# Another order table for the same 2,900 operations of a two-headed kernel (S4D convolution beside linear attention)

## The chip, the cores and the metric

One core of one Trainium2 chip. The metric is the device time in microseconds of one execution of the whole program. Of several runs the median counts. A profile is of one further execution, recorded instruction by instruction.

## The reference, cut to what matters

Two independent halves are computed from separate inputs and laid side by side in the output (2048 rows of 576 + 576 columns):

```python
# half A: a long convolution, by FFT of length 2*L, L = 2048, D = 576 channels, N = 128 states
dt = exp(log_dt);  A = -exp(log_A_real) + 1j * A_imag;  C = (C_real + 1j * C_imag) * dt
K = 2.0 * einsum("dn,dnl->dl", C, exp((A * dt)[:, :, None] * pos)).real
a = irfft(rfft(u.T, 2 * L) * rfft(K, 2 * L))[:, :L].T + u * D_skip
# half B: linear attention with H = 32 heads of 18
q, k, v = split(x @ wqkv)
phi = lambda y: concat([softmax(y @ w_phi), softmax(-(y @ w_phi))])
kv, z = phi(k).T @ v, phi(k).sum()
b = ((phi(q) @ kv) / (phi(q) @ z + 1e-6)) @ wo
return concat([a, b], -1)
```

## The kernel before, in words

All five engines work from one list of about 2,900 operations. `Plan.op` records each operation with its engine (some may run on either of two, ACT or DVE, DVE or POOL), its tiles and its dependences. Nothing is emitted then. At the end `pl.run(ORDER)` walks a long table of numbers, `ORDER`, and emits operation after operation. A number is an operation; `/7` after it names the buffer slot of a tile that the operation touches first, `*` takes the second engine, `!` sets a small activation first so that ACT's function table is loaded early, `+28` puts 28 warming matmuls in front. Each engine takes its instructions strictly in the order in which they were emitted, and waits at each for the tiles it reads and for the slots it writes. So the table decides four things: each engine's order, the order of the DMAs (all issued by SP), which engine takes an operation that has two, and which slot a tile lives in. The slots are few: 8 of PSUM (tile `ps`), 14 large ones (`zi`, `ac`, `x9`, `e`, `ks`, `E`), 19 of a row's size (`v1`, `o`, `ot`, `yo`, `ub`, `kb`, `us`, `zo`, `ff`, `fT`, `mx`), 7 small, 2 each for `pi`, `mg` and `cs`.

The work of half B:
- `fold` multiplies the key and query weights with `w_phi` (wkT or wqT blocks of 126 or 72 rows against the tile `fT` from wphi) and splits each result into a high part `wh` (ACT, L519) and a remainder `wl` (DVE, L520).
- `key_tile(t)`, t = 0 to 15, loads 128 columns of x (tile `zo`), splits them, makes three gemm outputs of 14 matmuls each, takes the two softmaxes (DVE maxima and minima, ACT exponential L598, POOL half sums L601, DVE L602 and L604, POOL product L467), and adds into the `kv` sums.
- `kv` transposes these sums and lays them out as blocks.
- `query_tile(t)` repeats the gemm and the softmax for the queries, transposes the features on TensorE (L705), multiplies them with the kv blocks, divides, transposes again (L735) and multiplies with wo in two halves.

The work of half A:
- `u_first` (16 blocks) is the first FFT stage of u: eight matmul pairs of a 64-row constant `w1` with the tile `kb`, four evictions to `zi`, two stores.
- `params` (6 blocks of 96 channels) prepares phases and angles in small DVE and ACT operations on tiles like `mx`, `mn`, `ax`, `pi`; `mags` does the magnitudes.
- Per pair of groups of four channels, `phases` sums up integers on POOL (L904, five times L908) into a `cs` slot, `waves` makes sines of them on ACT (L918, L925, L926), and `group` multiplies by magnitudes: three size matmuls (`ps` from `sel` and `mg`), exponentials on ACT (L942, L949), products on DVE and POOL, 64 small matmuls (`ps` from `E` and `cs`, L452), which free the `cs` slot, and sums into `ks` on DVE.
- After nine groups `k_first` does the first FFT stage of the kernel: the skip `dsk` is added to `ks`, and four blocks of matmuls (`ps` from `ks` and `w1`, each into four PSUM slots) are evicted to `zi`.
- `product` (16) is the middle of the FFT, the product of the spectra and the way back; `last` (16) is the last stage and the store.

Line 452 is the helper `mm`, through which nearly all matmuls go; lines 457, 460, 467 and 471 are helpers for copies and for products and sums. A TensorE instruction appears as a weight load (PEld) and a matmul (PE).

Of the kernel before, what the change touches and what calls it, by code (L numbers as in the profile page):

```python
# [285 lines left out]
482 1333 52* 1521 1339/1 1252 271/7 275/0 1475 1290/0/4/2/6/6 1514 43/7 53* 1330/8 1293 1207/6 1522 1291 1476 1294*
389 272/3 1328 44 1334 274 276/9 1523/11 278 1331/10 289*/8 1166 56/2 1292 1335 1477 1525 45 73 55/4 390 1336 1337
1340 61/1 1349/3 391/10 1255/0 62 273/7 277 1197/4 279 1518 63/4 59 212/9 58 60 1478 1524 64*/2 1341 1519/1 1351/7
1527 1354 65* 290 57/2 1533 213/10 1479 214* 1338 1520 1199/11 215* 1198 131/12 1347/13 239/14 381/7 240/7 241* 1526
1200/4/3/0/1/11 288 1237/15 1342 1343 1344 392/2 66 1352 1350 67/4 393/1 378/0 398 242* 280*/3 1203 394* 1239/14 132/0  # L290
1345 342/3 217/6 246/0 1204 133* 281* 450/10 1480 477/7 1528 1346 1390/0 395* 68/3 69/2 74 1432/1 1481 399 1529 1202*
218/1 1433 1389 245/3 158/11 70* 1348 1488/2/8/12 216/1 1434 261/4 1201* 1205 75* 1482 224/3 1484/4 1435 71* 1486/7
1483 270/2 221 220 223 54/3 222/13 225 1436 226/2 251/1 263 1489 76 1503/6/4/3 1491 1492 1437 282 262 283/1 1487 250
244/0 347/13 1530 243/4 235/9 1493 1531 1256 219/1 284/3 285/0 234 227 1485 1532 1534 134* 1698 1535/1 138/2 400 286*
228 1238 1536 229/12 348/5 1490 1494 1495/7/2/7 230/3 287 159/10 153/1 1537 1208/12 1538 1438 1504 349 1499/4 428/16
1699 155 247 248 1500 1507 1539 137/2 1540 135/5 252/8 249 253/2 1501/0 1541 231/4 232 254 429/12 1506 1496 1502
401/17 1497 1295 154 1227/15 350 1296 1505 1508 136/6 236 1498 1542 142/2 255 1509 143 237 256/13 1240/7/1/4/3/6 1439
1244* 140 1543 1544 1696 1440 1510/0 1511* 139 352/3 233 1242* 369/14 1177/18 1241 1206 1445/7/3/4 257/3 1545/1 141/11
1443/6 1441 144 258/4 1442 353/2 1217/2 1219/13 238 430* 291* 431 1547/0 1704 356/1 1512 1697 145*/0 1703 160* 1548
359 1705/9 1243 1446! 1447/4 1448 370 434/1 451 355 1549 1550 357/13 146* 147 1551 1451 161 162/6 1513 358 439/0 354/3  # L300
1450 1444 1453 1317/11 361/2 1552 1209* 435/4 1700 1449 1452 360 371 1245 1218 362 259 1246 1553 452 440 441/0
1210/2/7/6/3/1 1211 1214* 363 1213* 432/7 292 1220/2/4/1/0/9 1212* 1223 1707 1222 148/12 149/3 150/2 364/13 365/1 1221
1454/6 1460/4/3/4 1458/2 1461 1546 1462/1 1463 1459 260 264 1467 1466 151 1554 1224 156 366/5 1465 1555 496/16 152
163/7 1464 1468 367 1455* 1556 265 1706 1715 402/8 433/3 368* 1558/4/6/12 1562/2 1708 351/8 1557 455/6 456/5 185/2
1469/0 1709 1710 403* 436 1391/1 166/1 404 1559 1392 1456 1393 437 104/8 1457 442/2 438 1711 157 443 1563 1226 1470
167 168/11 1225 186/9 164/1 169 170 181 1560/3 1561 444 1257/4 1565 171 1394 1566 1395 408/6 425/17 172/2 1712
1575/2/3/4 1564 1471 405/9 1472 1576 1582 1568 1573/1 1583 406/7 1567 1577/0 1396 1216 1574 410/1 1397 445/1 446/0 173
372 407/4 457* 165/3 1701/0 412 458 174 1215 447/5 1178/6 187* 448* 1578 1398 1399 1713 409 1167/9 1579 449 1581 182
411/10 453 175/1 461/2 1404/1/8/1 413 415/5 1580 1402/3 414 1406/7 188* 416 1403! 320/13 466/1 454 1405 1714 1412
1569/0 1259/2 1584/6 1588/0 1589 1590 1411 1702 1570 1571 467 424 1716 1591 460/4 462/1 189/10 1407 1410 417 1717/10  # L310
176/5 478 1592 1258 1593 468/3 105/4 190/2 1400 1355 1572 177/0 1401 1408 178* 1421/3/6/12 423 106* 1718 107 321/0 464
418/10 463 465 1179 469*/5 479 1719 1417/1 179* 1720 1585 1586 1277/12 192/0 419/1 1587 420/2 109/4 1594 1419/6 183
# [24 lines left out]
629 1138/4 1011/4 1139/0 1907 630 631/8 1300/5/1/6/2/11 1301 1681/0 1304 1677/5 1302 1015 1140 1684 1016 536 1690 1678
1691 632/3 1742/1/3/6 1303 1141 1142 1686 1689 633 1147/7/4 537 1682 1687 1148 1145/6/16 1146 1143/2/8 1275 1688 1144
# [821 lines left out]
```

## Time and profile before

| | |
|---|---|
| median of 3 runs | 514.12 us (512.72 to 518.13) |
| the profiled execution | 511.75 us, its span 510.0 us |
| TensorE busy | 496.6 us, 97% of the span |
| DVE busy | 457.5 us, 90% |
| ACT busy | 396.8 us, 78% |
| POOL busy | 334.2 us, 66% |
| granted TensorE clock | 0.999 of full speed |
| moved by DMA | 115.95 MB, 227 GB/s |

The span runs from the first to the last instruction; the rest of the execution lies around it. Busy time of TensorE counts the union of its matmuls, which overlap. A row of the timeline gives the start, the duration, the engine, the source line, the operation, the tiles written and read, their shapes, how many equal instructions the row merges, and in brackets how long the engine had been idle and what ended that.

### The profile page before, as it was taken

The page shows a single profiled execution, that of the slowest core. Times are in us where ns is not written, and L with a number is a line of the kernel's source. Part 1 is how long each engine was busy: PE and PEld are TensorE (multiplying, and loading weights), DVE is VectorE, ACT ScalarE, POOL GpSimd, SP SyncE. Part 2 cuts the span into 40 slices and gives each one's busy share as a digit, 9 for nine tenths or more (in the row PEclk, how much of TensorE's full clock was granted, in tenths as well). Part 3 has the DMA queues.
Part 4 walks back from the last instruction along what each step waited for, and adds up shares of the span by engine and source line. Part 5 has one row for each costly group of instructions (what it writes and reads, how often), then busy time and mean ns, then how long its engine had stood idle before and what let it go on. Part 6 is the DMA issues. An engine that isn't in the chain of part 4 may idle for free.

```text
span 510.0 us, 20296 instructions
## 1 busy us (share of the span) xinstructions
PE 496.6 (97%) x8436; PEld 412.6 (81%) x8436; DVE 457.5 (90%) x1013; ACT 396.8 (78%) x683; POOL 334.2 (66%) x403
## 2 busy tenths in 40 slices
PE   7999999999999999899999999999999999999996
PEld 7799888999998879697887866776788886667976
DVE  4999999999899999999999999998989879789774
ACT  4699787999879989979989889899896445454331
POOL 1645697788987997995994569796554455634400
PEclk9999999999999999999999999999999999999999
DMA  7985947715137586781687965468986997998797
GB/s 212 333 294 178 330 143 252 235 57 170 59 121 254 149 257 207 212 275 58 211 239 255 286 180 181 147 219 272 293 269 213 347 274 219 321 311 295 260 314 193
DMA packets 80511, 115.95 MB, mean 227 GB/s; under 512 B 12452, under 2 KB 57636, under 8 KB 80420
## 3 DMA queue, kind: packets, MB, share of 16 engines
q1 hardware_dynamic: 80420, 114.67, 71.1%
q8 instruction: 66, 1.08, 0.9%
q14 instruction: 25, 0.20, 0.1%
HBM read 65.63 MB, written 49.01 MB: 225 GB/s over the span
## 4 chain that ended last, share of the span: by engine, by line
PE 80%; DVE 7%; ACT 6%; POOL 2%; DMA 2%; issue 2%; SPq 0%; POOLq 0%; DVEq 0%
PE ps L452 75%; PE ps L705 3%; PE ps L735 2%; POOL cs L908 1%; ACT cs L918 1%; DVE E L471 1%; DMA xd<-x 1%; DMA ub<-dram 1%; ACT e L598 1%; DMA fT<-in_wphi_dram 1%; POOL o L601 1%; DVE wl L520 1%; DVE e L467 0%; DVE zi L457 0%; DVE small L602 0%
## 5 line engine op out<-in xcount | busy, mean ns | idle before, releaser
L452 PE MATMUL ps<-wh,x 128*128 128x288 f32 (+2 forms) x1008 | 240.2, 318 | 1.0 <-ACT wh L519 0.4
L452 PEld LDWEIGHTS ps<-wh,x 128*128 128x128 f32 x1008 | 173.0, 188 | 11.8 <-issue 2.8
L452 PE MATMUL ps<-wl,x 128*128 128x288 f32 (+2 forms) x560 | 175.0, 313 | 0.0
L452 PEld LDWEIGHTS ps<-wl,x 128*128 128x128 f32 x560 | 105.3, 188 | 1.2
L908 POOL TENSOR_TENSOR cs<-cs,pi 128x64 int32<-128x64 int32 (+4 forms) x90 | 91.9, 1022 | 5.5
L601 POOL TENSOR_TENSOR o<-e 128x576 f32<-128x576 f32 x32 | 42.4, 1330 | 28.8 <-ACT e L598 22.3
L467 POOL TENSOR_TENSOR E<-v,cs 128x512 f32<-128x512 f32 x31 | 39.5, 1290 | 15.5 <-ACT v L949 12.6
L471 DVE TENSOR_TENSOR ac<-us,ps 128x576 f32<-128x576 f32 x64 | 44.8, 747 | 3.5 <-PE ps L452 2.5
L953 DVE TENSOR_TENSOR cs<-ps,cs 128x1024 f32<-128x1024 f32 x36 | 43.7, 1214 | 2.8 <-ACT ps L942 2.4
L942 ACT ACTIVATE ps<-ps 128x512 f32<-128x512 f32 x72 | 41.6, 591 | 5.1 <-PE ps L452 4.8
L598 ACT ACTIVATE e<-e 128x1152 f32<-128x1152 f32 x32 | 37.4, 1168 | 7.0 <-POOL e L467 4.8
L452 PEld LDWEIGHTS ps<-E,cs 128*32 128x32 f32 x2304 | 34.3, 110 | 10.5 <-issue 5.7
L467 POOL TENSOR_TENSOR e<-small,e 128x576 f32<-128x576 f32 x27 | 31.7, 1173 | 15.7 <-DVE small L467 10.7
L452 PE MATMUL ps<-sel,mg 128*128 128x512 f32 x108 | 40.4, 439 | 1.4 <-DVE e L471 1.0
L452 PE MATMUL ps<-E,cs 128*32 128x64 f32 x2304 | 40.1, 220 | 1.4 <-issue 0.6
L926 ACT ACTIVATE cs<-cs,hp 128x1024 f32<-128x1024 f32 x36 | 40.4, 1141 | 0.0
L925 ACT ACTIVATE cs<-cs 128x1024 f32<-128x1024 int32 x36 | 37.0, 1054 | 0.3
L918 ACT ACTIVATE cs<-cs 128x2048 f32<-128x2048 int32 x18 | 34.4, 1912 | 2.6 <-POOL cs L908 2.5
L457 ACT ACTIVATE zi<-ps 128x288 f32<-128x288 f32 x79 | 28.1, 414 | 8.4 <-PE ps L452 8.4
L467 POOL TENSOR_TENSOR e<-e,small 128x576 f32<-128x576 f32 x25 | 29.7, 1189 | 7.3 <-DVE small L467 6.6
L890 POOL TENSOR_TENSOR pi<-pi 128x192 int32<-128x192 int32 (+1 forms) x42 | 20.0, 486 | 18.9 <-DVE pi L886 16.8
L467 POOL TENSOR_TENSOR ac<-ac 128x288 f32<-128x288 f32 x24 | 19.2, 825 | 18.8 <-DVE ac L471 8.8
(146 smaller groups left out, 1050.0 us busy)
## 6 DMA issues: line engine op xcount, KB each, us to landing
dram<-zi SPq DMA_DIRECT2D x32, 288.0 KB, 4.8
xd<-x SPq DMA_DIRECT2D x16, 576.0 KB, 4.7
dram<-zi SPq DMA_DIRECT2D x16, 576.0 KB, 5.2
x<-xd SPq DMA_DIRECT2D x16, 576.0 KB, 5.6
kb<-dram SPq DMA_DIRECT2D x32, 288.0 KB, 4.6
ub<-dram SPq DMA_DIRECT2D x32, 288.0 KB, 6.2
dram<-zo SPq DMA_DIRECT2D x32, 288.0 KB, 4.4
zi<-dram SPq DMA_DIRECT2D x16, 576.0 KB, 8.8
```

What stands on the lines that cost most here:

```text
L452: pe.matmul(o, l, r, start=start, stop=stop, skip_group_check=skip)
L457: op(("act", "dve"), (c_act(n), c_dve(n)), lambda e: act.activation(dst(), src(), AF.Copy) if e == "act" else dve.tensor_copy(dst(), src() ...
L467: op(eng, [c_dve(n[0]) if e == "dve" else c_pool(n[1]) for e in eng], lambda e: (dve if e == "dve" else pool).tensor_tensor(dst(), a(), b( ...
L471: op(eng, c_dve(n) if eng == "dve" else c_pool(n), lambda: e.tensor_tensor(dst(), a(), b(), op=alu), r=r, w=w, with_=with_, lock=eng == "p ...
L598: op("act", c_act(1152) + 40, lambda: act.activation(e.t, e.t, AF.Exp), r=[e], w=[e], table="exp")
L601: op("pool", c_pool(517), lambda: pool.tensor_tensor(pair.t, e.t[:, :, :, 0:9], e.t[:, :, :, 9:18], op=ALU.add), r=[e], w=[pair], lock=True)
L908: op("pool", c_add(4 * n * W), lambda n=n, j=j: pool.tensor_tensor(x()[:, :, :, n:2 * n], x()[:, :, :, 0:n], pi.t[:, j:j + 2, gs].bitcast( ...
L918: op(("act", "dve"), (c_act(n) + 45, c_dve(n)), lambda e: act.activation(cs.t[:, 0], x(), AF.Abs) if e == "act" else dve.scalar_tensor_ten ...
L925: op("act", c_act(64 * W) + 150, lambda at=at: act.activation(at(1), at(1).bitcast(I32), AF.Sin, scale=TURN), r=[cs], w=[sine], with_=[cs] ...
L926: op("act", c_act(64 * W) + 225, lambda at=at: act.activation(at(0), at(0), AF.Sin, scale=-TURN, bias=hp.t), r=[cs, hp, sine], w=[both], w ...
L942: op("act", c_act(512) + 12, lambda: act.activation(ps.t, ps.t, AF.Exp), r=[ps], w=[ps], table="exp")
L953: op("dve", c_dve(64 * W), lambda: dve.tensor_tensor(F(), both(M.t), F(), op=ALU.mult), r=[M, ready], w=[long], with_=[cs])
```

## The change

`ORDER` is replaced by another table of the same 2,900 operations; nothing else changes. It came out of a search that set out from the current table, with the longest delays and the largest steps that the search allows. The first lines of both:

```diff
 ORDER = """
-180/0 33 0/0 1 1353 3 1358 2 1360 1362 72/1 1361 1366 396/2 1365 1368 1367/3 1369 1370 1371 1372 4/4 35+28/0 1359 1373
...
+369/0 1361 1360 1365 1366 1368 1367/1 1369 1370 1371 1372 1373 1353 0/0 2 450/2 3 477/3 374/4 375/1 1374 1375 4/5 1359
...
```

Operations move by 20 places on average. 174 of those with two engines take the other one: ACT has 643 operations in place of 636, DVE 1011 in place of 1013, POOL 394 in place of 399. Three places in rows; tiles carry the program's running numbers where the names alone would read alike.

SP's first DMAs, at the program's start. Before (tiles from `in_wkT` are weight blocks of the keys, `zo` from `in_xT` is an x tile, `fT` is wphi, the small ones are parameters of block 0):

```order
L508 DMA kvb_83<-in_wkT_dram 72x640
L843 DMA dt_94<-in_ldt_dram 128x96
L845 DMA cre_98<-in_cre_dram 128x96
L845 DMA cim_103<-in_cim_dram 128x96
L504 DMA fT_119<-in_wphi_dram 128x630
L845 DMA th_153<-in_aim_dram 128x96
L508 DMA e_175<-in_wkT_dram 126x640
L508 DMA ub_180<-in_wkT_dram 126x640
L508 DMA e_183<-in_wkT_dram 126x640
L495 DMA zo_185<-in_xT_dram 128x640
L508 DMA e_188<-in_wkT_dram 126x640
```

and now:

```order
L845 DMA cim_83<-in_cim_dram 128x96
L845 DMA cre_85<-in_cre_dram 128x96
L495 DMA zo_113<-in_xT_dram 128x640
L504 DMA fT_119<-in_wphi_dram 128x630
L845 DMA th_121<-in_aim_dram 128x96
L508 DMA kvb_126<-in_wkT_dram 72x640
L843 DMA dt_130<-in_ldt_dram 128x96
L508 DMA e_172<-in_wkT_dram 126x640
L508 DMA e_180<-in_wkT_dram 126x640
L508 DMA ub_182<-in_wkT_dram 126x640
L508 DMA e_212<-in_wkT_dram 126x640
```

The x tile `zo` goes out third in place of tenth, wphi fourth in place of fifth, the 72-row block `kvb` sixth in place of first.

TensorE from the end of query tile 12's gemm to query tile 15's products with kv (`ps` from `kb` is a block of `u_first`, from `sel` a size matmul, from `E` a group, from `ident` the transposes of query 15's features). Before:

```order
L452 MATMUL ps<-wl,x_3547 128x288
L452 MATMUL ps<-kb,w_246 64x288 x8
L452 MATMUL ps<-sel,mg 128x512
L452 MATMUL ps<-E,cs 32x64 x32
L452 MATMUL ps<-sel,mg 128x512
L705 MATMUL ps<-ident,e 128x128 x9
L452 MATMUL ps<-sel,mg 128x512
L452 MATMUL ps<-kvb,fT 64x76 x4
```

and now:

```order
L452 MATMUL ps<-wl,x_3251 128x288
L452 MATMUL ps<-kb,w_257 64x288 x8
L452 MATMUL ps<-sel,mg 128x512 x2
L452 MATMUL ps<-E,cs 32x64 x32
L452 MATMUL ps<-kb,w_257 64x288 x8
L452 MATMUL ps<-sel,mg 128x512 x2
L705 MATMUL ps<-ident,e 128x128 x9
L452 MATMUL ps<-sel,mg 128x512 x2
L452 MATMUL ps<-kvb,fT 64x76 x4
```

A second block of `u_first` (block 0, which stood before the gemm of query 15's second half) now stands ahead of the transposes. The size matmuls are sorted otherwise: two that stood ahead of the second half of query 12's gemm now follow the first block, and of the next group's one has moved behind the transposes and one from behind them ahead.

DVE around the second run of `k_first`, from the sums into `ks` to the evictions. Before (`zi` 4090 is filled from the first block of matmuls; `ks` 2528 and 2529 are the pair of kernel tiles):

```order
L471 TENSOR_TENSOR ks_2528<-ps_3906,ks_2529 128x32x4
L471 TENSOR_TENSOR ks_2528<-ps_4021,ks_2529 128x32x4
L471 TENSOR_TENSOR ks_2529<-ps_3777,ks_2529 128x32x4
L471 TENSOR_TENSOR ks_2528<-ks_2528,dsk_89 128x36
L471 TENSOR_TENSOR ks_2529<-ps_3906,ks_2529 128x32x4
L871 RECIPROCAL mx_4015<-mx_4015 128x96
L457 COPY ot_4008<-ps_4054 128x288
L590 TENSOR_REDUCE small_4104<-ps_3984 128x16
L471 TENSOR_TENSOR mn_4017<-mn_4017,mx_4015 128x96
L457 COPY zi_4090<-ps_4087 128x8x36
```

and now (`ks` 2529 and 2530; `zi` 4092 is filled from the first block, 4115 from the second):

```order
L471 TENSOR_TENSOR ks_2529<-ks_2529,dsk_100 128x36
L471 TENSOR_TENSOR e_4062<-ps_3998,small_4013 128x16x18
L471 TENSOR_TENSOR ks_2530<-ps_3793,ks_2530 128x32x4
L859 SCALAR_TENSOR_TENSOR mx_4066<-ax_3915,ay_3756 128x96
L471 TENSOR_TENSOR ks_2530<-ps_3917,ks_2530 128x32x4
L471 TENSOR_TENSOR x9_3992<-ps_3978,x9_3992 64x128
L471 TENSOR_TENSOR ay_3756<-ay_3756,ax_3915 128x96
L871 RECIPROCAL mx_4066<-mx_4066 128x96
L457 COPY zi_4092<-ps_4089 128x8x36
L471 TENSOR_TENSOR mn_4051<-mn_4051,mx_4066 128x96
L602 TENSOR_REDUCE small_4125<-o_3953 128x64
L457 COPY zi_4115<-ps_4114 128x8x36
```

The sum with `dsk` now stands ahead of the `mx` and `ay` of parameter block 4, and the first eviction `zi` ahead of the product `mn`.

More of the change, by code (lines that the diff above doesn't have):

```diff
@@ L286 @@
[L286 to L300, printed above, removed]
@@ L426 @@
[L426 to L428 removed]
+369/0 1361 1360 1365 1366 1368 1367/1 1369 1370 1371 1372 1373 1353 0/0 2 450/2 3 477/3 374/4 375/1 1374 1375 4/5 1359
+1 1377 33 376* 377* 1358 1362 1363/0 1364 1376 396/6 35+28/0 1378 12/2 1379/4 1380 1381 1382 38 5/3 19/7 34/1 36 37
@@ new lines @@
+429/0 1440 1240/1/3/7/2/1 1507 233 143 144 270/5 1357 1207/10 1317/7 159/4 257/1 1543 1242 1544 160* 1219/6 1244
+145*/2 430* 1441 1241 1277/14 1510/6 1511 401/15 402/9 1705/1 1443/2/5/8 354/3 431 355/4 237* 1547/0 1442 356 258/0
+1447/1 432/6 1448! 1548 1549 291* 1697 357/13 1550 146* 1450 1696 1551 353/0 358 99/11 1243 1245 359 1545 1512 238
+1445/7 1446 1444 1451 371 360 1452 147 1453 370 1208*/18 1552 1553 1449 1209* 1513 1700 259* 351/7 361*/2 362 434/4
+451* 435/3 452 1210/6/2/0/7/12 292 1707 440/4 423/10 1211 1218 1213* 439 441/2 1214 1212 363 148/9 161* 1454/6
@@ new lines @@
+1689 492 1147/4/10 1148 494 493 495 1145/6/18 1143/0/17 1691 2034 1907 1908 1286 634 635 1742/4 1690 1740/1 1146
+1152/6 1018/3 2042 1687 1144 1149/0 2038 1153/4 535/1 1745 1679 1154/17 1150/0 1680 1151 538/11 2035 1019 536 1741
+1692/2 537 2066/1 539 1747 1952/1 1953 640/6/18 1748 641 1746 636/7/10 540 1954 637 1955 638/0/11 1155/6/5 639
+1757/7/6/0 1156/1 1157 1956 1743 1749 1158 1755/3 1750 2036 1159 645/0 1756 642/1 1758 646/0 1759/6 1760 643/4 1957
+1306 1761 2041 1751/4 647/10 1020 1021/11 644 1763 1161/5 697/10 1910/0 1762 648/1/0 1227/18 1228*/10 1163/17 1765
@@ new lines @@
+1866/6/4/0/7/6 704 2060 2219 1971* 1869* 1867* 2061 1868* 703 1917 1164 1920 1973 1032/2 1870* 1871 1035/0 1970*
+1980/4/10/5 705 1033/3 706/0 1036/4 1188*/12 1034/5 855/6 859/3 1872/1/7/3/5/1 1037 1918 860 1875* 1974/0/4/13 1921
+1189* 707 1873* 861/2 1975* 1976 1919 1981 1876* 1175 1038/3/2 1309* 1039/7 1977 2062 2063 2064 1982/6 1983/5 1986*
+1874 1040 1041 854/1 708 1988 892/3 1877 1042 856 857 1230/7/3/6/0/6 1232 1978/2 1979 1985* 1987 858 1231 1234 1233
+1236 709/10 1043/5 1045/5 1310/6/0/7/1/12 1984 862*/4 2224 1989/2 863 1235 1314 710/2 711 1311 1190/6/1/5/4/1
@@ new lines @@
+870/1/12 2069 2225/17 2497/18 871 873* 2470/3/0/6/2/8/7 728 729 876/5 2471 2474* 2473 1047 2070 2071 730 2001 2227
+877/4 2477/2/4/1/3/9/11 2480 2481 2072 874/6/12 2472 2478 875 2226 2235 2228 2073 731/7 733*/7 878/5 2536/3/6/1/0/3/4
+2539* 2540* 2074 732/2 2538 2479 734* 2076 2425/9 2229 2537 2541/6 2543/4/6/0/1/2/10 2075 2221/1 2077 2544
+2482/5/7/2/3/8/2 2484 2446/14 2545 879/4 2006/6/9/11 2486* 2547 940*/4 2230 2231 2546 2004/7 2005 2485 2008/3 894/1
+2019/2/6/1 880/0 881 657 882/4/0 2009/4 2512/15 2010 893/7 2222 2407/16 2007 941 2013 2014 2020 883/7 2023/6 942
@@ new lines @@
+2238 2239 2099 2114 2115 2240 2241 2117 582/6 581/5 586/0 2085* 2116 2454/7 2100* 587 584 588/12 902 2101*
+2526/3/0/2/1/10/15 2527* 583 2242 2118 2487 2528* 2095/4 2096 585 2530* 589/2 590 2089/6 2090* 2529* 957/0 958/3
+2448/5/3/7/1/17/13 2451 2091 959 2092 2452 2450 2102 2449 2554 2103 2453/8 2243 2244 2455/6/0/2/7/2/10 903 736/0 2456
+2121/3/1/6 2122 2245 2246 2457 2123/5 2124/7 2126* 2459 2127* 2119/4 2128 2129 2120 2164/1/5/8 2491/12 2104/6 2490/2
+2165/17 2498/5 2105 591 592/8 2249/0 904/7 2458 888/0 2489/3 2125 890 960/3/1 961/7 2423/11 2492/2/7/5/0/13/14 962
@@ new lines @@
+2260/5 2332 2156* 2333 2158* 2155* 2263! 594 2504/4/3/0/2/14/17 910* 2265/0 2261 2270 2506 2505* 2266 2279/1/4/11
+2398/5 2507* 2431/18 911/7/3 912* 913/4/12 914* 2334 2269 2335 543/3 2336 2147 548 547 2508 595 2280/6
+2426/7/0/5/1/8/1 2430* 2399/4 2429* 2282* 2337 915/6 2555/9 918/1 2427* 916/3 549 2338 2268* 550/4 2433/7/5/4/2/3/9
+919/5 917/3 2510 2267* 2271/3 596 597/6/13 2428 2436 2435 2339 2437 551 599/4/18 920 2275/5 2340 2434 2276 600 2281
+2277/1 2283* 2278 2284 2285 598 552 553/17 2272 2401/2/0/7/4/8/6 2405* 921/6/5 2403 2404 2509 2273 2159 2402* 922/5
@@ new lines @@
+1076/3 2739/3/1/7/5/4/10 2815 792/4/15 2742 1073 2805 2806 2709 2741 2633/16 2671 2672 2808 2746/0/6/2/7/6/5 2740*
+793* 2641/7 2743 2752 2580/5/1/3/4/9/5 2583 2632/2 794/7/11 2751 2753* 2754 2582 2764/10 984 795 2807 2747 2584 692/2
+694/18 2634/17 2581* 2748 2749* 2587/5/4/0/7/13/2 2588 2640/4 2750 2677/6/1/3/2/0/1 2681 2589 798/5 2762/8 2595 2678
+2680 985* 986 2590 2679 2683 2755/3/4/6/2/9/15 2759 2758* 796/0/14 797 2682 2757 693/1 2596 2591 2597 2763/6 695
+2635/7/4/0/6/5/1 2637 2636 801/1 2756* 2761 799/4 2592 2593* 800/16 2770/17 802/4 803 2639* 2771/11 2638
@@ L429 @@
+852 1121/1 1123 1125
 """.split()
```

242 lines of the change are left out of this document (110 added, 132 removed).

## The prediction

> **What bounds the kernel now.** I read the page first (busy time, granted clock, the chain), then busy time by stage, then the rows of the three places where TensorE waits.
>
> ```profile
> span 510.0 us, 20296 instructions
> PE 496.6 (97%) x8436; PEld 412.6 (81%) x8436; DVE 457.5 (90%) x1013; ACT 396.8 (78%) x683; POOL 334.2 (66%) x403
> PEclk9999999999999999999999999999999999999999
> ...
> 5.76:15.36 9.60, 8.90 (x51) 8.19 (x51) 6.77 (x21) 6.07 (x16) 3.37 (x7) 1.00 1.01 293
> 15.36:66.00 50.64, 49.58 (x484) 45.37 (x484) 49.86 (x102) 42.23 (x66) 30.80 (x43) 1.00 0.84 280
> 66.00:165.00 99.00, 98.79 (x1734) 90.14 (x1735) 95.73 (x208) 88.48 (x137) 82.53 (x101) 1.00 0.49 157
> 165.00:204.00 39.00, 38.89 (x797) 32.76 (x798) 37.72 (x85) 37.00 (x59) 34.60 (x42) 1.00 0.70 205
> 204.00:245.00 41.00, 38.47 (x600) 32.06 (x598) 39.84 (x92) 37.18 (x65) 33.98 (x39) 1.00 0.62 187
> 245.00:310.00 65.00, 64.19 (x1295) 51.09 (x1295) 61.03 (x143) 57.94 (x98) 47.70 (x56) 1.00 0.77 236
> 310.00:371.00 61.00, 60.08 (x1354) 43.27 (x1354) 56.12 (x117) 55.81 (x95) 46.92 (x52) 1.00 0.69 220
> 371.00:505.85 134.85, 134.61 (x2133) 106.83 (x2101) 109.29 (x248) 69.69 (x149) 53.48 (x60) 1.00 0.86 277
> ```
>
> The stage rows give length, then busy time of PE, PEld, DVE, ACT and POOL. TensorE has work in 97% of the span, at full clock. An order can't shorten that work; it can only shorten the time in which TensorE has none. From 5.76 to 505.85 us the stages leave it idle for 0.70 + 1.06 + 0.21 + 0.11 + 2.53 + 0.81 + 0.92 + 0.24 = **6.6 us**. Matmuls overlap, so a wait shorter than one of them (about 0.3 us in the rows below) hardly shows; I take as much again for these, an estimate. So all that an order can win inside is 6.6 us shown and perhaps 13 us in truth. The largest piece stands at 204 to 245 us. From 66 to 204 us there is next to nothing to win (0.32 us), though DVE is busy for 133.5 of 138 us there: an order can lose in that stretch, not gain.
>
> What lies outside is a start and an end:
>
> ```profile
> 505.52 0.29 PE L452 MATMUL ps<-wl,x 128*128 128x288 f32 x1
> 505.85 0.41 ACT L457 ACTIVATE ot<-ps 128x288 f32<-128x288 f32 x1 [1.43 <-PE ps L452]
> ```
>
> After the last matmul come one eviction and the last store, 510.0 - 505.85 = 4.15 us. The change ends with the same two gemm halves and the same eviction: **0**. The profiled execution took 511.75 us (510.0 span and 1.75 around it); the median of the runs is 514.12, 2.37 above. I sum against 511.75 and add the sum to 514.12.
>
> **The head: SP's first issues.** The first real matmul needs wphi (tile fT) and the first block of wkT (kvb).
>
> ```profile
> 0.74 0.44 SPq L508 DMA_DIRECT2D kvb<-in_wkT_dram  x1
> 2.60 0.43 SPq L504 DMA_DIRECT2D fT<-in_wphi_dram  x1
> 4.88 0.38 SPq L495 DMA_DIRECT2D zo<-in_xT_dram  x1
> 5.76 2.38 PE L452 MATMUL ps<-fT,kvb 72*128 72x72 f32 x10 [0.97 <-DMA fT<-in_wphi_dram]
> 12.41 0.68 DVE L520 TENSOR_TENSOR wl<-ps,wh 128x504 fp32r<-128x504 f32 x1 [0.38 <-ACT wh L519]
> 12.68 0.59 ACT L519 ACTIVATE wh<-ps 128x504 fp32r<-128x504 f32 x1 [0.18 <-PE ps L452]
> 13.15 1.84 PE L452 MATMUL ps<-fT,e 126*128 126x126 f32 x12 [0.28 <-DVE wl L520]
> 15.36 0.41 PE L452 MATMUL ps<-wh,x 128*128 128x378 f32 x1 [0.37 <-ACT wh L519]
> ```
>
> SP issues one DMA about every 0.46 us here (2.60 to 4.88 in five steps). wphi moves from fifth to fourth, 0.46 earlier; kvb moves from first to sixth, so it goes out near 0.74 + 5 x 0.46 = 3.0 us, 0.4 later than wphi did, which was the later of the two. The first x tile (zo, 128 x 640 floats, 0.33 MB) now goes out third, ahead of every weight: at the 293 GB/s of this stage it costs the weights behind it 1.1 us. So the first fold comes 0.4 to 1.5 us later. But the last wkT block stands eleventh in both orders, behind the same ten transfers. Its ten folds are the end of the run at 13.15, so it had landed by about 13.6. TensorE spent the time from 5.76 on blocks that landed one by one, and a later start eats that waiting. The first gemm (15.36) needs the remainders wl of the first three wkT blocks of 126 rows. The third now stands tenth, one before the last: I place its landing at 12.4 and its folds at 13.8, a block after it; ACT's 0.59 and DVE's 0.68 make 15.1. I take **0**, with -0.5 and +1.5 as ends.
>
> **Place A, query tile 15 (205 to 214 us).**
>
> ```profile
> 193.67 5.20 POOL L908 TENSOR_TENSOR cs<-cs,pi 128x64 int32<-128x64 int32 x5
> 198.90 1.91 ACT L918 ACTIVATE cs<-cs 128x2048 f32<-128x2048 int32 x1
> 204.96 1.28 ACT L949 ACT_TABLE_LOAD   x1
> 207.51 1.18 ACT L598 ACTIVATE e<-e 128x1152 f32<-128x1152 f32 x1
> 209.08 0.43 ACT L457 ACTIVATE zi<-ps 128x288 f32<-128x288 f32 x1
> 208.83 1.31 POOL L601 TENSOR_TENSOR o<-e 128x576 f32<-128x576 f32 x1 [1.03 <-ACT e L598]
> 212.70 0.32 ACT L457 ACTIVATE ks<-ps 128x128 f32<-128x128 f32 x1
> 212.24 1.17 POOL L467 TENSOR_TENSOR e<-e,small 128x576 f32<-128x576 f32 x1
> 208.56 1.72 PE L452 MATMUL ps<-kb,w 32*64 32x288 f32 x16
> 212.00 0.51 PE L452 MATMUL ps<-sel,mg 128*128 128x512 f32 x1
> 213.47 1.20 PE L705 MATMUL ps<-ident,e 128*128 128x128 f32 x9 [0.96 <-POOL e L467]
> ```
>
> The transposes at 213.47 wait for a chain that began at 193.67: POOL's phases of the next group pair, ACT's sines for them, a table load, only then the softmax exponential at 207.51, and POOL's two passes over it. TensorE's own work in that time is shorter than the chain, so its rows from 208.56 on stand apart. The change keeps the steps of the chain in this order on POOL and ACT; one size exponential takes the place of an eviction ahead of the softmax, 0.3 us. TensorE has the same work ahead of the transposes: one size matmul goes behind them and another comes ahead, one u block moves here from further up, and the two kv transposes move behind the group matmul that frees POOL's buffer. A stall that a chain sets doesn't shrink by sorting what stands under it: **0**. Below it may be -0.5, if the buffer comes free earlier. Above it is +1.0: the u block's four evictions, of which DVE had two, are now all on ACT (0.43 each) behind the softmax, and the size matmuls ahead of the transposes need their slots. Nine ACT instructions stand between the exponential and the first of them; nine took 5.2 us before (207.51 to 212.70), so the first starts near 213.0 and the second ends near 213.6.
>
> **Place B, the second key FFT block (228 to 239 us).**
>
> ```profile
> 230.98 1.25 PE L452 MATMUL ps<-ks,w 32*128 32x288 f32 x16 [0.36 <-DVE ks L471]
> 234.28 1.74 PE L452 MATMUL ps<-ks,w 32*128 32x288 f32 x16
> 229.06 5.18 POOL L908 TENSOR_TENSOR cs<-cs,pi 128x64 int32<-128x64 int32 x5
> 232.38 1.98 DVE L471 TENSOR_TENSOR mn<-mn,mx 128x96 f32<-128x96 f32 x1
> 234.29 0.45 DVE L457 COPY zi<-ps 128x288 f32<-128x288 f32 x1
> ...
> L471 DVE TENSOR_TENSOR mn<-mn,mx x6: 245/251/1982, 6.3 to 279.8; 128x96 f32<-128x96 f32 x6
> ```
>
> The second block (234.28) needs PSUM slots that the first one filled. Their eviction (zi at 234.29) stands on DVE behind mn, which took 1.98 us where its kind takes 0.251, until POOL's run of five ended at 234.24. The second block took 1.74 against 1.25, and the first began 0.36 late. In the change DVE adds dsk to ks before the reciprocal's relatives mx and ay, the eviction stands ahead of mn, and the second block writes slots that older tiles left. I follow it by rows: the ks sums end 0.1 to 0.3 earlier, the first block starts at 230.8, the second at 232.5 when ACT has emptied the last slot, both gemm halves behind it run without a wait, and a size matmul waits 0.45 for the first block's last eviction, still behind mn. The same work ends at 238.4, not 239.0: **-0.6**. Ends: -1.8 (all three waits go) and +0.4 (ACT's sines hold the slot as long as mn did).
>
> The Trainium skill's page "SBUF — State Buffer", section "SBUF: two separate sides", says that a DVE instruction with two SBUF inputs and a GpSimd instruction that reads SBUF exclude each other for a whole instruction. The 1.98 us that end with POOL's run agree. By that rule mn is stretched again in the changed kernel, and the sum is the -0.6 above; if the stretch were chance, mn would take 0.25 and the sum would be -1.0.
>
> **The rest.** ACT gets 7 instructions more, DVE 2 and POOL 5 fewer: 3 us of evictions for ACT, which is idle for 113 us. SP's order changes most among the loads for the products of the first half; the tightest of them, product 0's second ub, still follows the matmuls of product 1 that free its slot. For all other places I take **0**: 6.6 - 0.70 - 2.53 = 3.4 us of shown idling could be won, and as much lost.
>
> Sum: 0 (end) + 0 (head) + 0 (A) - 0.6 (B) + 0 (rest) = **-0.6**: 511.2 for a profiled execution like this one, **513.5** for the median.
>
> **Rivals.**
> - *Most of the waits go.* The stages with waits (15 to 66, 204 to 371 us) give back 1.06 + 2.53 + 0.81 + 0.92 = 5.3, and a fifth of the hidden ones 1.3: -6.6, 507.5. For it: 6.6 us is there, and each is a wait of the kind an order can cure. Against it: the largest, place A, is a chain that the order leaves as it was.
> - *ACT becomes what TensorE waits for.* Place: 165 to 245 and 310 to 371 us, where ACT is busy 37.00 of 39, 37.18 of 41 and 55.81 of 61. Evictions moved to it, as at A, queue behind sines and exponentials. It decides from the point where the second of A's moved evictions ends after the softmax is ready, 213.4 us; then every microsecond counts. Price: all four evictions and the 0.3 late, 4 x 0.43 + 0.3 = 2.0 us a stage, 6 in three: 520.1. For it: my count at A is 213.6. Against it: only there do I see it, for 0.2 us.
> - *Nothing at all.* The moves are small (most operations shift by a few places) and fall where TensorE never waited: 514.1.
>
> **How the numbers follow.** About 1% (5.1 us) is what a measurement of this kernel can tell from no change. My forecast with its own range, 510.5 to 516, has 0.45, nothing at all 0.16 within it or just beside it, the waits going 0.22, ACT 0.17. That gives faster 0.22, same 0.61, slower 0.17. The range reaches into both outer cases, 506 to 519.5.
>
> **What would show it.** Right: TensorE's first row with wh stays within 0.5 us of 15.36; the transposes of query 15 still wait for POOL e, near 213 us; the second ks block starts less than 1.6 us after the first; the idle sum of the stages is 5.5 to 7. Wrong: a DMA release of more than 1 us inside the stages after 245 us, ACT as the releaser of PE's longest waits, or an idle sum under 3 or over 10.

## The result: 518.02 us, 0.85% slower, and the profile after

| | before | after |
|---|---|---|
| median of 20 runs each | 513.89 us (510.12 to 518.13) | 518.02 us (514.89 to 522.53) |
| ratio, 95% interval | | 1.0085, 1.0062 to 1.0107 |
| the profiled execution, its span | 511.75, 510.0 us | 516.81, 515.0 us |

On two other chips the ratio was 1.0059 (1.0031 to 1.0086) and 1.0042 (1.0011 to 1.0074). The change makes the kernel slower by 2 to 4 us; I had forecast 0.6 us less.

The page of after, its summary, and busy time by the stages used ahead of it (length, then PE, PEld, DVE, ACT, POOL; the last stage is longer by what the kernel lost):

```profile
span 515.0 us, 20244 instructions
PE 490.9 (95%) x8436; PEld 410.5 (80%) x8436; DVE 453.4 (88%) x1011; ACT 398.4 (77%) x690; POOL 334.8 (65%) x398
...
5.76:15.36 9.60, 6.29 (x57) 6.39 (x58) 4.32 (x17) 5.79 (x12) 2.62 (x6) 1.00 0.94 251
15.36:66.00 50.64, 50.09 (x412) 47.06 (x415) 48.86 (x106) 41.81 (x69) 30.08 (x39) 1.00 0.83 288
66.00:165.00 99.00, 98.51 (x1745) 90.64 (x1734) 96.04 (x210) 88.64 (x138) 80.72 (x99) 1.00 0.46 145
165.00:204.00 39.00, 36.44 (x876) 30.21 (x862) 35.61 (x78) 35.82 (x60) 32.58 (x35) 1.00 0.65 194
204.00:245.00 41.00, 38.54 (x593) 32.96 (x595) 39.14 (x93) 37.99 (x70) 33.72 (x43) 1.00 0.62 181
245.00:310.00 65.00, 64.76 (x1307) 51.74 (x1301) 61.71 (x141) 59.18 (x99) 50.36 (x56) 1.00 0.79 245
310.00:371.00 61.00, 57.57 (x1310) 41.03 (x1310) 53.91 (x116) 54.39 (x91) 44.85 (x50) 1.00 0.68 213
371.00:511.00 140.00, 138.51 (x2211) 110.52 (x2199) 112.68 (x255) 72.61 (x153) 58.98 (x65) 1.00 0.88 279
```

TensorE now idles for 3.31 + 0.55 + 0.49 + 2.56 + 2.46 + 0.24 + 3.43 + 1.49 = 14.5 us, where it was 6.6. Three stages carry most of the rise: the head, 165 to 204, and 310 to 371 us; the last stage adds 1.25.

Idle time alone misses matmuls that start late but overlap. So I matched TensorE's operations of two traces by their numbers in the program, gave each the time that its kind usually takes, and read at equal sums of that work by how many us a kernel stood behind the first profile of before. The first column says when before got there; the three columns on the right are experiments told below (the other slot, the head of before, both):

```
before at    after  again  third   before  | slot   head   head+slot
   us       (three profiles)       again   | (e3b)  (e5)   (e11)
  22.7       2.90   4.34   2.90    1.90    |  2.36   0.94   0.08
  87.0       0.62   2.07   0.64    1.84    |  0.08  -0.36  -1.13
 175.3       1.56   2.85   1.43    4.64    |  0.87   0.27  -0.51
 202.3       4.08   5.43   4.11    5.47    |  3.91   3.03   2.18
 259.6       2.20   3.89   2.39    4.72    |  2.10   1.50   0.59
 350.8       2.05   3.34   1.91    6.20    |  1.36   1.00   0.41
 357.8       4.49   4.56   3.84    6.28    |  1.55   2.87   0.69
 437.2       3.38   3.56   2.72    5.39    |  0.56   1.80  -0.49
 503.2       5.33   4.85   4.63    7.44    |  1.99   3.05   0.85
```

The three profiles of after agree by place: 3 to 4 us lost in the head, about 2.2 won back until 87 us, 2.5 lost between 175 and 202, 1.5 to 1.9 won between 202 and 260, 1.2 to 2.4 lost within 7 us at 355, about 1 won until 437, and 1.3 to 2 lost after that. The column "before again" is the same kernel as the reference of the table, in another execution: this is how far two executions of one program lie apart, and why medians of many runs, not one profile, carry the verdicts below.

Not every step of the table belongs to the change, since the first profile of before was a quick one. I read other profiles in the same way: before again, and those of the experiments that keep before's order at a place. At 22.7 us nine profiles with before's head stand at -0.5 to 1.9 us, seven with after's head at 2.4 to 4.8. From there to 87 us before's order wins at most 0.1. Between 175 and 202 us it loses -0.2 to 1.4, after's order 2.4 to 3.0; between 202 and 260 us it wins 0 to 0.8, and at 355 us it loses nothing. Behind 358 us, though, before's order does as after's does: 0.9 to 1.2 won until 437, 1.5 to 2.2 lost after that. So the five steps that I named up to 358 us are the change's, at least in part; they add up to 3.5 to 4.3 us in the three profiles. The last two steps are not.

**The head.** TensorE's first row in before:

```profile
1.67 3.12 PE L227 MATMUL ps<-ident,zero 128*128 128x126 bf16 x28 [1.67 <-DVE zero L487]
```

and TensorE's rows of after:

```profile
9.07 3.10 PE L227 MATMUL ps<-ident,zero 128*128 128x126 bf16 x28 [9.07 <-DVE ident L485]
11.97 1.43 PE L452 MATMUL ps<-fT,kvb 72*128 72x72 f32 x10
18.68 0.44 PE L452 MATMUL ps<-wh,x 128*128 128x378 f32 x1 [0.28 <-DVE wl L520]
```

and DVE's of after:

```profile
5.88 0.26 DVE L471 TENSOR_TENSOR mn<-mn,mx 128x96 f32<-128x96 f32 x1
7.83 0.26 DVE L859 SCALAR_TENSOR_TENSOR ax<-ax,ay 128x96 f32<-128x96 f32 x1 [1.69 <-ACT ax L849]
8.06 0.18 DVE L1001 MEMSET dsk<- 128x144 f32 x1
8.21 0.11 DVE L487 MEMSET zero<- 128x64 uint32 x1
8.63 0.26 DVE L859 SCALAR_TENSOR_TENSOR ax<-cre,ax 128x96 f32<-128x96 f32 x1 [0.31 <-ACT ax L849]
8.80 0.22 DVE L485 TENSOR_SCALAR ident<-x 128x128 f32<-128x128 int32 x1
```

The 28 warming matmuls read `ident` and `zero`, and every fold stands behind them in TensorE's order. DVE makes both in 0.3 us, but they now stand behind parameter instructions that wait for ACT, which waits for loads, and `ident`, the tenth on DVE, ends at 9.0 us. In before, the warming ran at 1.67, hidden under the loads. The first gemm moves from 15.36 to 18.68 us.

**The slot at 355 us.** ACT and TensorE in the timeline of after, and below them, from its chain of work, the store that ACT waits for:

```profile
350.45 0.73 ACT L457 ACTIVATE us<-ps 128x288 f32<-128x288 f32 x2
352.43 0.89 ACT L460 ACTIVATE x<-ps 128x512 fp32r<-128x512 f32 x2 [1.25 <-DMA dram<-zi]
...
353.81 0.50 PE L452 MATMUL ps<-sel,mg 128*128 128x512 f32 x1 [0.19 <-DVE x L471]
355.08 0.47 PE L452 MATMUL ps<-sel,mg 128*128 128x512 f32 x1 [0.77 <-ACT zo L457]
...
357.94 0.78 PE L452 MATMUL ps<-kvb,fT 128*64 128x76 f32 x16 [1.32 <-DVE small L724]
```

```profile
344.60 7.75 DMA dram<-zi
```

The tile x of query 9 (a transposed output that ACT fills) sits in large slot 5, whose owner before it was a `zi` of the third `k_first`. That tile's store is issued at 344.60 and lands 7.75 us later. Until then ACT stands still, with the evictions that DVE and TensorE wait for behind it.

**Places A and B.** TensorE in after, at query 15's transposes and at the second `k_first`, and there DVE's `mn` and the last of POOL's phase instructions:

```profile
213.50 1.10 PE L452 MATMUL ps<-E,cs 128*32 128x64 f32 x64 [0.73 <-DVE E L471]
215.83 0.80 PE L452 MATMUL ps<-sel,mg 128*128 128x512 f32 x2 [0.55 <-ACT zi L457]
216.53 1.31 PE L705 MATMUL ps<-ident,e 128*128 128x128 f32 x9
...
234.87 2.33 PE L452 MATMUL ps<-ks,w 32*128 32x288 f32 x32
...
236.58 0.25 DVE L471 TENSOR_TENSOR mn<-mn,mx 128x96 f32<-128x96 f32 x1
...
236.62 2.11 POOL L908 TENSOR_TENSOR cs<-cs,pi 128x1024 int32<-128x1024 int32 x1
```

The transposes wait for nothing now; the two waits ahead of them come to 1.28 us. Both `ks` blocks run in one piece of 2.33 us, and `mn` takes 0.25 us.

### The profile page after: what moved, and what is told of

The parts are those of the page before. It is cut to its first block, busy times and chain, and to the rows that moved or that the text cites. A ratio compares the mean times of both kernels' runs of the same rounds, so it can differ in the third digit from the quotient of the medians.

```text
span 515.0 us, 20244 instructions
## 1 busy us (share of the span) xinstructions
PE 490.9 (95%) x8436; PEld 410.5 (80%) x8436; DVE 453.4 (88%) x1011; ACT 398.4 (77%) x690; POOL 334.8 (65%) x398
## 4 chain that ended last, share of the span: by engine, by line
PE 39%; DVE 5%; DMA 5%; ACT 4%; issue 2%; POOL 2%; SPq 0%; DVEq 0%; ACTq 0%; POOLq 0%
PE ps L452 35%; DMA dram<-zi 2%; PE ps L705 2%; DMA ub<-dram 1%; DMA dram<-zo 1%; PE ps L735 1%; DVE ac L471 1%; ACT zi L457 1%; POOL kb L467 1%; DVE zi L457 0%; POOL pi L890 0%; DVE zo L457 0%; ACT x L460 0%; DVE cs L953 0%; ACT cs L926 0%
## 5 line engine op out<-in xcount | busy, mean ns | idle before, releaser
L908 POOL TENSOR_TENSOR cs<-cs,pi 128x64 int32<-128x64 int32 (+4 forms) x90 | 90.8, 1009 | 5.3
L601 POOL TENSOR_TENSOR o<-e 128x576 f32<-128x576 f32 x32 | 44.2, 1381 | 30.9 <-ACT e L598 24.3
L467 POOL TENSOR_TENSOR E<-v,cs 128x512 f32<-128x512 f32 x34 | 43.3, 1290 | 14.7 <-ACT v L949 14.4
L467 POOL TENSOR_TENSOR e<-small,e 128x576 f32<-128x576 f32 x24 | 28.8, 1200 | 13.3 <-DVE small L467 12.4
L467 POOL TENSOR_TENSOR e<-e,small 128x576 f32<-128x576 f32 x26 | 31.2, 1201 | 8.7 <-DVE small L467 8.1
L457 ACT ACTIVATE zi<-ps 128x288 f32<-128x288 f32 x85 | 29.8, 412 | 8.0 <-PE ps L452 8.0
L467 POOL TENSOR_TENSOR ac<-ac 128x288 f32<-128x288 f32 x27 | 21.6, 828 | 20.9 <-DVE ac L471 18.6
```

The costliest lines, as they stand in the source:

```text
L457: op(("act", "dve"), (c_act(n), c_dve(n)), lambda e: act.activation(dst(), src(), AF.Copy) if e == "act" else dve.tensor_copy(dst(), src() ...
L467: op(eng, [c_dve(n[0]) if e == "dve" else c_pool(n[1]) for e in eng], lambda e: (dve if e == "dve" else pool).tensor_tensor(dst(), a(), b( ...
L601: op("pool", c_pool(517), lambda: pool.tensor_tensor(pair.t, e.t[:, :, :, 0:9], e.t[:, :, :, 9:18], op=ALU.add), r=[e], w=[pair], lock=True)
L908: op("pool", c_add(4 * n * W), lambda n=n, j=j: pool.tensor_tensor(x()[:, :, :, n:2 * n], x()[:, :, :, 0:n], pi.t[:, j:j + 2, gs].bitcast( ...
```

## The experiments

Sixteen runs in four groups; each group ran on one chip of its own, beside before. In the diffs, numbers are operations of the table. An interval is about 0.3% wide to either side.

**Ident first.** In after:

```diff
-369/0 1361 1360 ... 1353 0/0 2 450/2 3 ... 1359 1 1377
+369/0 0/0 2 1 1361 1360 ... 1353 450/2 3 ... 1359 1377
```

> The table of after with three operations moved to the front: POOL's iota, DVE's memset of zero and DVE's ident, which the warming matmuls and so the first fold wait for. In after TensorE's first gemm starts at 18.68 us, in before at 15.36. Both theories: the first fold at 6 us in place of 11.97, the first gemm near 15.5. Theory 'the head stays': DVE is busy for 98% of 16 to 86 us, so what is lost ahead of it is never won back; the 3.2 us come off the whole time, 518.0 to 514.8. Rival 'the head is absorbed': the same share of TensorE's work is done only 0.7 us later in after than in before at 78 us, so the lead fades until then; 518.0 to 517.3, and the rest of the loss lies elsewhere.

517.02 us, ratio 1.002 (0.999 to 1.005). The timeline:

```profile
1.51 3.10 PE L227 MATMUL ps<-ident,zero 128*128 128x126 bf16 x28 [1.51 <-DVE ident L485]
7.68 2.38 PE L452 MATMUL ps<-fT,kvb 72*128 72x72 f32 x10 [3.08 <-DMA kvb<-in_wkT_dram]
10.96 4.63 PE L452 MATMUL ps<-fT,e 126*128 126x126 f32 x20 [0.90 <-DMA e<-in_wkT_dram]
18.30 0.44 PE L452 MATMUL ps<-wh,x 128*128 128x378 f32 x1
```

Both theories missed the head itself: the first gemm is at 18.30, not near 15.5. With `ident` out of the way the next thing is late, the loads: `kvb` and the 126-row blocks stand behind the x tile. The two tables of this group that keep after's head whole (below) start their gemm at 20.34 and later, and this one stays 2.0 us ahead of them up to 169 us. The times don't show that: 517.02 stands beside 517.28 and 516.30 of these two.

**Ident late, in before.**

```diff
-180/0 33 0/0 1 1353 3 1358 2 1360 ... 4/4 35+28/0 1359 1373 ... 1375 1376
+180/0 33 0/0 1353 3 1358 1360 ... 4/4 1359 1373 ... 1375 2 1 35+28/0 1376
```

> The table of before with DVE's memset of zero and ident moved behind its tenth parameter instruction (the ax of L859 that reads cre), as in after, and nothing else. Both theories: the first fold waits until about 12 us, the first gemm starts near 18.5. 'The head stays': before + 3.2, 517.1, ratio 1.006. 'The head is absorbed': before + 0.7 at most, 514.6, ratio 1.001.

522.75 us (6 runs), ratio 1.0136 (1.0095 to 1.0177), more than either theory gave. The gemm starts at 20.04 us, and the lag behind the first profile of before is 5.3 us at 22.7 us and 5.3 at 259.6: in this table a late head stays, and nothing is absorbed. The part above 5.3 came behind 260 us, where before again falls back as well.

**The other slot.** In after, large slots 5 and 6 exchanged from operation 922 on:

```diff
-922/5 ... 658/6
+922/6 ... 658/5
```

> The table of after with large slots 5 and 6 exchanged from the feature tile x of query 9 on; the order is untouched. In after that tile sits in the slot of a k_first tile zi whose store lands only at 352.4 us, so ACT stands still for 1.25 us in front of it, DVE 1.59 behind ACT, and TensorE waits 0.19, 0.77 and 1.32 us from 353.8 to 357.9. Theory 'each wait counts': ACT starts the tile near 351.2, the three waits of TensorE shrink to about half a us, and the whole time falls by 1.3 to 2.4, to about 516. Rival 'given back later': what follows is bound by DMA (share 0.88 after 371 us), so the waits go and the time stays at 518.

516.30 us, ratio 0.9996 (0.9965 to 1.0026), in a group without after itself. So it was run again beside after:

> The kernel of after once more, as the measure for the three beside it on this chip. Both theories: ratio 1.006 to 1.0085.

> The slot exchange alone, again, now with after itself on the same chip. Theory 'each wait counts': 2.0 us (0.4%) faster than after, ratio 1.002 to 1.0045. Rival 'given back later': as after, 1.006 to 1.0085; its first ratio of 0.9996 was then the chip's.

After 517.95 us (1.0042, 1.0011 to 1.0074), the other slot 516.89 us (1.0029, 0.9998 to 1.0061). The timeline of the second run:

```profile
350.56 0.94 ACT L460 ACTIVATE x<-ps 128x512 fp32r<-128x512 f32 x2
352.99 0.74 PE L452 MATMUL ps<-sel,mg 128*128 128x512 f32 x2
355.00 0.79 PE L452 MATMUL ps<-kvb,fT 128*64 128x76 f32 x16 [0.21 <-DVE small L604]
```

ACT no longer waits, TensorE's three waits shrink to 0.21, and the lag grows by 0.2 us across this place in place of 1.9 in after of the same group (1.36 to 1.55, against 1.91 to 3.84). The medians differ by 1.06 us; the intervals overlap, so of the time alone the second group tells the slot only as 0 to 0.3%. Shown is the wait and its cause: in the seven profiles with after's slot at this place the lag grows there by 1.2 to 2.4 us, in the seven with the other slot by 0.1 to 0.6.

**The kv transposes.** Two repairs of the stretch from 175 to 202 us. In the first, ACT's split 533 goes behind the four evictions of folds and the transposes (487, 489 and the copy 490) behind `u` block 1270:

```diff
-533 ... 514 ... 487/4 1661 489/2 490*/1 ... 1270/7/5/0/1/5
+514 533 ... 1661 ... 1270/7/5/0/1/5 487/4 489/2 490*/1
```

> The table of after with ACT's split of the first wo piece (L535, which waits 1.59 us for its load at 190.8 us) moved behind the four evictions of folds that stand behind it, and with the two kv transposes moved behind the next u block on TensorE. Theory 'each wait counts': the u block starts near 194.6 in place of 196.93 behind the transposes, TensorE's wait of 1.66 us at 195.97 falls to about 0.4, and the time falls by 1.3, to 516.7. Rival: DVE, busy for 35.6 of 39 us here, is what the fold's evictions wait for, so TensorE waits elsewhere for as long and the time stays at 518.

517.28 us, 1.0027 (0.9996 to 1.0057). The lag grew by 2.7 us across the stretch, as in after: the rival held. In the second, POOL's products of key tile 1 (98, 102) go ahead of the phases, with its matmuls (103) and the copy of the sums (486) behind them:

```diff
+97 98 102 1655/1 ...
-98 ... 102 103 ... 486/11
+499/2 103 486/11 ...
-487/4 ... 489/2 ... 1270/7/5/0/1/5
+487/5 ... 489/1 ... 1270/7/4/0/2/5
```

The diff leaves out one more changed slot, of 1127.

> The table of after with the two products of key tile 1 on POOL (the k features and v) moved ahead of the six phase instructions of group pair 5, the key tile's 64 matmuls and the copy of the kv sums moved up behind them, and the kv transposes in two slots that are free by then. Theory 'POOL's order': TensorE reached key tile 1's matmuls at 192.66 us because v came at 192.6, behind 5.1 us of phases; now they run near 188, the kv transposes no longer wait for DVE (1.66 us), DVE not for them (1.22), and the time falls by 1.2 to 2.5. Rival: the phases come 2.4 us later, ACT's sines behind them, and the gemm and group work that follows waits for those: no gain.

517.63 us, 1.005 (1.002 to 1.0079), after in this group 517.90. The lag grows by 1.7 us there in place of 2.6; the time does not follow.

**After again, and the head of before in it.** The first 87 operations in the order, on the engines and in the slots of before (slot numbers behind them renamed):

```diff
-369/0 1361 1360 1365 1366 1368 ... 1165 42
+(memsets of v1) 33 0/0 1 1353 3 1358 2 1360 1362 1361 ... 41 42
```

> The kernel of after, beside the others of this group on one chip, with a profile of its own. Theory 'the loss is in the order': ratio 1.0085 to before as first measured, and its head like that of the two tables with after's head that ran before it (first gemm near 20.5 us, where the first profile of after had 18.68). Rival 'the machine differs': ratio under 1.004, and then the gains of the first experiments are smaller than they look against 1.0085.

> The table of after with its first 87 operations in the order, on the engines and in the slots that before gives them (slot numbers behind them renamed to fit); from there on after's own order. Theory 'the head stays': the lag behind before after the first folds and gemm (2.9 to 4.5 us) goes entirely, nothing gives it back, ratio 1.0085 less 0.006 to 0.009, about 1.001. Moving ident alone had taken 2.0 us of it: the rest, then, is the x tile that goes out ahead of the weights. Rival 'only ident': what loads ahead is needed soon anyway, so the ratio stays near 1.004.

After 517.90 us, ratio 1.0059 (1.0031 to 1.0086); with the head of before 515.52, ratio 1.0012 (0.9984 to 1.0040): 0.47% less, 2.4 us. The two intervals overlap a little; seven of its twelve runs are faster than the fastest of after's twelve (515.77). The first gemm starts at 15.98 us in place of 20.12. Of the 3.4 us that the head then leads by, 1.8 are left at the end.

> The head of before, POOL's key products first and the other slot for query 9's tile, all three in the table of after. Theory 'they add': the gains of the single ones add up, 3 to 4.5 from the head, 1.2 to 2.5 from POOL's order, 2.4 from the slot, so that it beats before by 2 to 5 us: ratio 0.990 to 0.996. Rival 'they overlap': the last stage, where DMA is busy for 0.88, ends all of them alike, and the ratio stays at 0.997 to 1.001.

All three repairs: 513.90 us, 0.9987 (0.9954 to 1.0019), 4.0 us under after in the same group. It doesn't beat before; in its profile TensorE waits 1.89 us at 423.89 for a `kb` load, longer than for any load in the other profiles behind the head.

**The eviction ahead of mn, in before.**

```diff
-2047 1858 1856*
+1858 1856* 2047
```

> The table of before with one operation moved: at the second key FFT block DVE's product mn goes behind the first eviction into zi. It does alone what the prediction's place B rests on. Theory 'the stretched mn sets the second block': the eviction starts near 232.4 us in place of 234.29, the second block of ks matmuls near 233 in place of 234.28, TensorE's three waits there (0.36, the gap ahead of the block, 0.52) shrink by 1.2 in sum, and the time by as much, ratio 0.998. Rival 'ACT's slot': ACT empties another slot of that block no earlier than DVE did, the block moves by less than 0.4 us and the time by nothing.

514.51 us, 0.9991 (0.9955 to 1.0028). TensorE, DVE and POOL at the place:

```profile
232.65 1.25 PE L452 MATMUL ps<-ks,w 32*128 32x288 f32 x16 [0.37 <-DVE ks L471]
235.94 1.25 PE L452 MATMUL ps<-ks,w 32*128 32x288 f32 x16
237.83 0.50 PE L452 MATMUL ps<-sel,mg 128*128 128x512 f32 x1 [0.64 <-DVE e L471]
...
234.05 0.44 DVE L457 COPY zi<-ps 128x288 f32<-128x288 f32 x1
234.41 1.61 DVE L471 TENSOR_TENSOR mn<-mn,mx 128x96 f32<-128x96 f32 x1
...
230.72 5.19 POOL L908 TENSOR_TENSOR cs<-cs,pi 128x64 int32<-128x64 int32 x5
```

The eviction runs ahead, and the second block takes 1.25 in place of 1.74 us; but it still starts 3.3 us after the first, since half a gemm stands between the two on TensorE. The lag falls by 0.35 us over the place: the rival held. Even that may be chance. In before again, without any edit, `mn` took 0.66 us, the second block 1.25, and the lag falls by 0.9 us there (5.85 to 4.91 between before's 225 and 247 us). Its `mn`, and the POOL instruction that ran when `mn` started:

```profile
237.53 0.66 DVE L471 TENSOR_TENSOR mn<-mn,mx 128x96 f32<-128x96 f32 x1
...
236.91 1.16 POOL L908 TENSOR_TENSOR cs<-cs,pi 128x512 int32<-128x512 int32 x1
```

**Two tables joined.** Before up to operation 1136 (202 us), after with the other slot behind it; then before again from 2514 (430 us); and before once more:

> The first 1136 operations (to about 202 us) as before has them, the rest in the order of after, with the other slot for query 9's tile. Theory 'places add up': the table of after loses 2.9 to 4.3 us in its head and 2.6 between 175 and 202 us, and wins back 2.2 between 50 and 87 and 1.5 between 202 and 260; with the two losing stretches gone and the slot repaired, what follows 202 us is worth -1.0 to -2.7 us up to 430 us and +1.3 behind it: ratio 0.997. Rival 'the end decides': the stores and loads of the last stage end both tables alike, ratio 1.000 or above.

> As the run ahead, and from operation 2514 on (about 430 us) the order of before again. Theory 'places add up': without the 1.3 us that the order of after loses in the last stage, ratio 0.994 to 0.995. Rival 'the end decides': 1.000.

> The kernel of before beside the others of this group, for a second profile of it on this chip: it shows which of its places differ from one execution to the next. Ratio 1.000 by construction. If the theory 'the first profile was a lucky one' holds (its 511.75 us is 2.4 under the first median), TensorE waits 1 to 3 us longer in it than in the first, behind 240 us, where loads and stores are waited for; otherwise it repeats the first to within 0.5 us at each place.

514.74 us, 1.0003 (0.9974 to 1.0032); 516.22 us, 1.0024 (0.9990 to 1.0059); and before against itself 516.51 us, 1.0027 (0.9995 to 1.0060). No place's gain shows. Before's profile of this group is the column "before again": an execution of 519.17 us, the slowest of its twelve. The two longest rows among TensorE's waits in it (us in total, times, longest; "issue" is nothing that the profile shows), and below them the row of "issue" in the first profile of before:

```profile
PE ps L452 <- issue: 4.4, 7, 0.9
PE ps L452 <- DMA ub<-in_wkT_dram: 2.4, 1, 2.4
```

```profile
PE ps L452 <- issue: 0.6, 1, 0.6
```

**Head and slot; and the middle.**

> The head of before and the other slot in the table of after. Theory 'they add': 0.47% and 0.4% less than after, ratio 0.998 to 1.000. Rival 'they overlap': as the head alone, 1.001 to 1.003.

> As the run ahead, with the operations from 918 to 1136 (about 170 to 202 us) also in the order of before. Theory 'the stretch costs': TensorE lost 2.6 us there against before in both profiles of after; without it the ratio falls by 0.4 to 0.5% more, to 0.994. Rival 'it is won back': the gain behind it (1.5 us between 202 and 260) is the same work caught up, so the ratio stays at that of the run ahead.

Head and slot: 513.49 us, 0.9990 (0.9954 to 1.0026), 4.5 us under after (517.95) beside it by the medians, 2.7 (0.52%) by the ratios to before. Eight of its twelve runs are faster than the fastest of after's twelve (515.77). With the operations from 918 to 1136 in before's order as well: 518.89 us, 1.0058 (1.0023 to 1.0093). The lag grew by 2.4 us between 162 and 175 us and 4.1 between 175 and 202, where that of head and slot grew by 0.35 and 2.7; TensorE's two longest waits were of 2.0 us for DVE's `e` and 1.5 for its `zi`. Most of the loss, 5.4 us, lies between 172 and 180 us, where the piece begins. Whether before's order meets tiles there that after's order finishes at other times was not tried, so this run doesn't say what before's order is worth in the stretch.

## Why the prediction was wrong

The forecast of -0.6 us, no change to speak of, missed the direction; 518.02 lies inside the range of 506 to 519.5 only because the range was made wide enough for the rivals.

- **The end**, 0: about right. From the last eviction to the end of the span it is 3.8 us in after, 4.15 in before.
- **The head**, 0 with -0.5 and +1.5 as ends: this is the step that failed. The first gemm moved by 3.3 us in the profile of after, 4.8 and 3.3 in the two others. The sentence that the first real matmul needs wphi and the first block of wkT left out the warming matmuls ahead of it, and so `ident` and `zero`. I read SP's order and priced the loads, and did not ask what else the first matmul needs. The page had the answer in before, where TensorE's first row is released by DVE's `zero`; DVE's order in the change shows `ident` tenth. The loads were also under-priced: with `ident` first, `kvb` is waited for until 7.68, 1.9 us later than the first fold of before where I had 0.4 to 1.5, and the gemm starts at 18.30 us. Either cause alone gives 18.3 (loads) or 20.0 (ident, in before's table); both together 18.2 to 20.6 in seven profiles. So they overlap: removing `ident` alone brought no gain that the times show, and the loads alone were not tried. The sentence that a later start eats the waiting for blocks was wrong for this size: the late head in before's table stayed whole at 5.3 us until 260 us. In after's table some of a lead fades (3.4 to 1.8 us).
- **A**, 0 with -0.5 and +1.0: about right in size (the lag grows by 0.2 to 0.6 us between before's 202 and 225 us), wrong in its reason. The transposes no longer wait for POOL; the group's matmuls and a size matmul ahead of them wait instead, for DVE (0.73) and for an eviction on ACT (0.55).
- **B**, -0.6 with -1.8 and +0.4: the right sign, under-sized. Between before's 225 and 247 us the lag falls by 1.9 us in all three profiles of after, just beyond my end of -1.8; in before again it falls by 0.9 without any change. Moving the eviction alone gave 0.35. For the rest I can only point at the order around it, in which both blocks stand together; no run took that apart. That `mn` is stretched again was wrong: it took 0.25 us there, ahead of POOL's last phase instruction, not 1.98.
- **The rest**, 0 with 3.4 either way: held as a range, not as a value. The slot at 355 us is an ACT wait of the kind that my slower rival named, but through a store that holds a slot, not through sines and exponentials; it cost 1.2 to 2.4 us in the profiles. I had named stretches where an order can only lose, 66 to 204 us; the loss of 2.5 us at its end is that.
- **My signs**: the gemm left its 0.5 us, the transposes did not wait for POOL, the idle sum came out as 14.5, over 10, and ACT waited 1.25 us for a DMA at 352 us. These four said wrong. One sign of right held: the two `ks` blocks stand in one piece of 2.33 us, so the second starts less than 1.6 us after the first. The sign of the gemm was too narrow in any case: in nine profiles with before's own head it starts between 14.7 and 17.6 us.

Shown by runs: head and slot together take 4.5 us off after by the medians, 2.7 by the ratios, and it then measures as before does; the head alone takes 2.4, with intervals that just overlap. Open: the 2.5 us between 175 and 202 us, which three edits did not recover in time, and why the joined tables do not add up. What after seems to lose in the last stage, other profiles of before lose too.

## What to carry to other kernels

Before an order is judged, list what the first matmul needs, all of it: constants made on the chip and warming inputs too, not loads alone. A slot number is part of the order: a tile placed behind a tile that is still being stored makes a whole engine wait for that store. Places of one order don't carry over into another piece by piece, and against executions that differ by 7 us a single profile says where time goes but not how much. Two or three profiles of the kernel before tell which differences belong to the change.

## What the runs showed of the hardware that I had not expected

Two executions of the same program, before, had spans of 510.0 and 517.4 us at a granted clock of 0.999 and 0.997; TensorE's waits for nothing that the profile shows came to 0.6 us in one and 4.4 us in seven pieces in the other, and for a weight load in the head TensorE waited 2.4 us in the other and not at all in the first. A store of 0.59 MB took 7.75 us from issue to landing with other transfers around it; the median of the sixteen stores of this kind in after is 4.8. DVE's `mn`, 0.25 us by itself, was stretched to 1.98 us (before), 1.97 (ident late in before), 1.61 (the eviction ahead of it) and 0.66 (before again). Each time it ended about 0.1 us after the one POOL phase instruction that was running when it started: the last of the run in the first three (ends at 234.24, 239.58 and 235.91 us), the last but one in before again (236.91 + 1.16 = 238.07). In the three profiles of after it started just ahead of the last and longest, and took 0.25. The section "SBUF: two separate sides" of the Trainium skill's page "SBUF — State Buffer" describes such an exclusion for whole instructions; these rows agree with it.
